# Last two experts' rows gathered in quarters and turned by VectorE, second-layer conversions moved, wider planned steps for the later searches

## The chip, the cores and the metric

One core of one Trainium2 chip runs the whole program. The metric is device time in microseconds (us), the median of several executions. TensorE (PE), VectorE (DVE), ScalarE (ACT), GpSimd (POOL) and SyncE (SP) each run their own queue of instructions in order; a DMA is issued from SP's, ACT's or POOL's queue.

## The reference

Eight heads of causal retention (attention scores with a decay in place of a softmax) give 4608 rows of 512, and a mixture of eight experts works on those rows. Each token goes to one expert, by a greedy walk over all logits from the largest down, 576 tokens per expert.

```python
scores = scale * np.matmul(q, k.transpose(0, 1, 3, 2))      # B, H, S, D = 8, 8, 576, 64
ret = scores * Dmat[None]                                   # Dmat = gamma ** (i - j), i >= j
x = np.matmul(ret, v) ... reshape(4608, 512)
...
order = np.argsort(-(x @ w_gate).flatten())
for idx in order:
    tok, e = int(idx) // E, int(idx) % E
    if assigned[tok] >= 0 or counts[e] >= cap:              # cap = 576
        continue
    assigned[tok] = e; counts[e] += 1
...
for e in range(E):
    mask = assigned == e
    out[mask] = np.maximum(x[mask] @ w1[e], 0.0) @ w2[e]    # 512 -> 1024 -> 512
```

## The kernel before

The first 165 us or so compute the retention and the logits; the rows x are written to a buffer `xd` in HBM. The rest is the mixture, and only this is changed.

**Routing.** The sort is replaced by searches. Phase p (0 to 7) finds the p-th expert to fill up and its 576 tokens. `search` narrows a threshold in seven steps: VectorE makes a table G (line 173), PE counts with it (nine matmuls, line 346, into `r`), VectorE turns the counts into the next table. Then `members` (PE line 414, after a scan `sc` on VectorE, line 405), `listing` (PE line 452, result `idx`: five columns of 128 row numbers) and `leave`, which strikes the tokens out. These phases run beside the experts' matmuls, one or two experts ahead.

**Experts** are numbered 0 to 7 in the order in which the phases find them. `gather` fetches an expert's rows from `xd` by five indirect DMAs on POOL's queue, 128 rows of 2048 bytes each (64 in the last). `transposes` turns them: per 128 rows four PE transposes into PSUM (line 942), a copy `xh` rounded to fp32r on ScalarE (944), and the remainder `xl` by a subtraction on VectorE (945). Weights come as `raw` tiles by SP; `conv` splits one into a high part (ScalarE, 910) and a low part, for which ScalarE writes the negated high part of it (914) and an accumulating DMA on POOL's queue adds `raw` (915). Four conversions of W2 stand in layer 1 of their own expert, four of W1 of the next expert in layer 2.

**Layer 1** (`l1`): 16 groups i = 0 to 15 of 12 matmuls (line 973), over 256 and 320 tokens in turn. ScalarE evicts a group as `hb` (977), VectorE makes its remainder (980). **Layer 2** (`l2`): five tiles of tokens, each in eight steps; a step is three matmuls of 512 columns (line 1014), in the last tile of 64 tokens two. `scatter` writes a tile to the output by an indirect DMA on POOL's queue. So an expert has 192 + 112 = 304 matmuls.

**Order.** The order on each engine is fixed when the program is written, by `Mixer`: `t` is a planned time of PE that `adv` moves on with every three matmuls, `v` a planned time of VectorE; a phase yields how long VectorE needs before its next PE instructions, multiplied by `slack` (1.0 for p < 2, else 1.2), and these are put into PE's queue when `t` has come so far. In layer 2 a step counts 650 ns in every tile.

Of the kernel before, what the change touches and what calls it, by code (L numbers as in the profile page):

```python
# [10 lines left out]
F32 = mybir.dt.float32  # L11
F32R = mybir.dt.float32r
BF16 = mybir.dt.bfloat16
I32 = mybir.dt.int32
ALU = mybir.AluOpType
AF = mybir.ActivationFunctionType
# [3 lines left out]
NP, HP, NB = 4, 4, 9  # L20
N, DM, E, FF = 4608, 512, 8, 1024
SLACK = 1.0

def consts_np():
    h = np.arange(H); g = (1.0 - 2.0 ** (-5.0 - h)).astype(np.float64)
# [61 lines left out]
class Route:  # L87
# [333 lines left out]
    def listing(s, p):  # L421

        nc, V, pool, ps = s.nc, s.nc.vector, s.pool, s.ps
        q = s.q
        lb, hb = pool.tile([128, 36, 2], BF16, name="lb"), pool.tile([128, 36], BF16, name="hb16")

        V.tensor_scalar(hb, q, 1.5*2**28, 1.5*2**28, op0=ALU.add, op1=ALU.subtract)
        two = lambda a: a[:, :, None].to_broadcast([128, 36, 2])
        V.scalar_tensor_tensor(lb, two(q), HALF, two(hb), op0=ALU.add, op1=ALU.subtract)

        rh = pool.tile([128, 3, 20, 36], BF16, name="rh")
        lc = ps.tile([128, 168], F32, name="r")
        lp, cn = lc[:, :160].rearrange("p (v x c) -> p v x c", v=2, c=4), lc[:, 160:]
        early = 0 < p < E - 1
        w = 4 if p else 2
        if early:
            s.taken()
        for g0, g1 in ((0, 9),) if p else ((0, 5), (5, 9)):
            c, n = slice(4*g0, 4*g1), 4*(g1 - g0)
            V.tensor_tensor(rh[:, 2, :, c], s.i20[:, :, c], hb[:, None, c].to_broadcast([128, 20, n]), op=ALU.is_equal)  # L440
            s.reach(4*g0, 4*g1, 32, lb, ALU.is_equal)
            if p:
                V.tensor_scalar(rh[:, 1, :, c], rh[:, 2, :, c], s.pc, None, op0=ALU.mult)
            else:
                nc.scalar.activation(rh[:, 1, :, c], rh[:, 2, :, c], AF.Copy, scale=s.pc)
            V.tensor_tensor(rh[:, 0, :, c], rh[:, 2, :, c], s.cc[:, :, c], op=ALU.mult)
        if not p:
            s.idle(9)
        for g0, g1 in ((0, 9),) if p else ((0, 5), (5, 9)):
            yield (2500 if not p else 3700 if early else 2780), (75 if p else 110)*(g1 - g0)  # L450
            for c in range(4*g0, 4*g1, w):
                nc.tensor.matmul(lp[:32*w, :, :, :w], s.G[:, c:c+w].rearrange("p c k -> p (c k)"), rh[:, 0:2, :, c:c+w],
                                 start=(c == 0), stop=(c + w == 36), skip_group_check=True)
        if early:
            nc.tensor.matmul(cn, s.ones, s.n8, start=True, stop=True, skip_group_check=True)
        if early:
            s.room(cn)
        s.idx = pool.tile([128, 5], I32, name="idx", bufs=8)
        lo = pool.tile([32, 2, 2, 20], F32, name="lo")
        own = [lp[32*c:32*c+32, :, :, c] for c in range(4)]  # L460
        for c in range(w//2):
            V.tensor_copy(lo[:, c], own[c])
        for a, b in ((0, own[2]), (1, own[3]), (0, lo[:, 1])) if w == 4 else ((0, own[1]),):
            V.tensor_tensor(lo[:, a], b, lo[:, a], op=ALU.add)
        for a in range(4):
            V.scalar_tensor_tensor(s.idx[32*a:32*a+32], lo[:, 0, 0, 5*a:5*a+5], 128.0, lo[:, 0, 1, 5*a:5*a+5], op0=ALU.mult, op1=ALU.add)

    def taken(s):

# [390 lines left out]
def moe(tc, nc, P, R, xd, w1_d, w2_d, out, mix):  # L860
    V, A, T = nc.vector, nc.scalar, nc.tensor
    ident, warm = P['ident'], P['warm']
    found = []
    ready = lambda k: len(found) > k
    regs, XG = {}, {}
    state = dict(dma=0, conv=0, most=2, listing=-1)
    RAW, W1, W2, XH, XL = {}, {}, {}, {}, {}
    scat = []
# [1 line left out]

    def phases():
        for p in range(E):
            mix.slack = 1.0 if p < 2 else 1.2
            if p < E - 1:
                yield from (R.search() if p else R.search_first())
                regs[p] = nc.sync.value_load(R.e[0:1, 0:1], min_val=0, max_val=E - 1)
            state['listing'] = p
            yield from R.members(p)
            if p == E - 1:
                regs[p] = nc.sync.value_load(R.e[0:1, 0:1], min_val=0, max_val=E - 1)  # L880
            yield from R.listing(p)
            found.append(R.idx)
            if p == 0:
                yield 0, 0
            if p < E - 1:
                yield from R.leave(p)

    def dma_pump():

        while state['dma'] < min(state['conv'] + 4, 8*E):  # L890
            e, k = divmod(state['dma'], 8)
            if e not in regs or state['dma'] >= state['most']:
                return
            t = P['raw']()
            src = (w1_d if k < 4 else w2_d)
            nc.sync.dma_start(t, src[bass.ds(regs[e], 1), :, (k % 4)*1024:(k % 4)*1024+1024].rearrange("a p x -> (a p) x"))
            RAW[e, k] = t
            state['dma'] += 1
# [18 lines left out]
        state['conv'] += 1  # L917
        dma_pump()

    def gather(e):  # L920
        if e in XG or not ready(e):
            return
        xg = P["c"].tile([128, 5, DM], F32, name="xg", tag="xg")
        for j in range(5):
            n = 128 if j < 4 else 64
            nc.gpsimd.indirect_dma_start(out=xg[:n, j, :], out_offset=None, in_=xd[:, :],  # L926
                                         in_offset=bass.IndirectOffsetOnAxis(ap=found[e][:n, j:j+1], axis=0))
        XG[e] = xg
        state['arrives'] = mix.t + 9000

    def transposes(e):

        xg = XG[e]
        xh = P['w'].tile([128, 4, 576], F32R, name="xh", bufs=1)
        xl = P['w'].tile([128, 4, 576], F32R, name="xl", bufs=1)
        XH[e], XL[e] = xh, xl
        for j in range(5):
            n = 128 if j < 4 else 64
            tag = ("t", "h0", "h1", "h0", "h1")[j] if e else ("t", "y", "y", "t", "y")[j]
# [9 lines left out]
    def l1(e, tr):  # L949
# [4 lines left out]
            order[:8] = [(f, s) for s in range(2) for f in range(4)]  # L954
        for i, (f, s) in enumerate(order):
            wh, wl = [w.rearrange("p (f d m) -> p f d m", f=2, d=4)[:, f % 2] for w in W1[e, f // 2]]
            if i == 0 and e:
                next(tr, None)
                next(tr, None)
            elif e == 0 and i in (1, 2):  # L960
                next(tr, None)
            elif i in (1, 3):
                for _ in tr:
                    pass
            xh, xl = XH[e], XL[e]
# [16 lines left out]
            mix.vec(340 + 140*s)  # L982
            if e == 0 and i == 4:
                state['most'] = 8*E
            if i in ((3, 5, 9, 13) if e else (3, 5, 7, 9, 11, 13)):
                conv()
        return hb

# [8 lines left out]
    def l2(e, hb):  # L997
# [41 lines left out]
            conv()  # L1039
        if e + 1 < E and e + 1 not in XH:  # L1040
            mix.drain(lambda: ready(e + 1))
            gather(e + 1)
            tr = transposes(e + 1)
        return tr

# [24 lines left out]
    run.regs = regs  # L1070
    return run

def build(tc, nc, qk, vk, cst, wg, rf, w1, w2, out):
    with ExitStack() as top:
        P = {}
        P['c'] = top.enter_context(tc.tile_pool(name="c", bufs=1))
# [21 lines left out]
        with ExitStack() as ctx:  # L1098
# [15 lines left out]
                if what:  # L1114
                    warm(what)
            R.idle = idle
            run = moe(tc, nc, P, R, xd, w1, w2, out, mix)
            mix.drain(lambda: 0 in run.regs)
            while rows:
                rows.pop(0)()  # L1120
# [21 lines left out]
```

## Time and profile before

| | us |
|---|---|
| median of 3 runs | 637.7 (636.39 to 641.17) |
| profiled execution | 638.66 |
| its span (first to last instruction) | 636.9 |
| PE / DVE / ACT / POOL busy | 606.7 / 394.4 / 265.5 / 222.7 |

The span and all busy times are of the one profiled execution; 1.76 us of its time lie outside the span. Matmuls overlap, so a busy PE is not a PE at its peak: a row's duration (0.39 us for a matmul of 512 columns) is longer than the distance to the next one.

### The profile page before, as it was taken

Reading aid. Unit: us, or ns where it says so; the run is one execution under the profiler, and the core shown is the slowest. Engines: PE = TensorE matmul, PEld = TensorE weight load, DVE = VectorE, ACT = ScalarE, POOL = GpSimd, SP = SyncE. Lnnn points to the kernel's source line nnn. Section 1 sums busy time; section 2 is a strip of 40 time slices with the busy share of each in tenths; the row PEclk is TensorE's granted clock in tenths of the full one; section 3 lists DMA queues with packets and bytes.
Section 4 is the critical chain, followed back from the end, with each engine's and each line's share of the span. In section 5 each row is a group of like instructions: output and inputs, shape, how many; then the busy total and the mean of one; then the engine's idle time right before and its main releaser. Section 6 shows DMA issues by size and latency. Waiting matters only on the chain.

```text
span 636.9 us, 14773 instructions
## 1 busy us (share of the span) xinstructions
PE 606.7 (95%) x5758; PEld 520.1 (82%) x5762; DVE 394.4 (62%) x1444; ACT 265.5 (42%) x455; POOL 222.7 (35%) x268
## 2 busy tenths in 40 slices
PE   7999999998899999999999999979999999999995
PEld 5888888765598779878977987879789889889973
DVE  2466788788789878878976996878682203302300
ACT  1333333342364445543562465155415724734510
POOL 4887374600311352251432323151323224131111
PEclk9999999999999999999999999999999999999998
DMA  8999898934667597894897399467938986893521
GB/s 328 410 381 373 283 392 259 365 106 142 199 162 170 184 248 179 235 240 140 210 226 233 81 234 241 125 148 189 249 118 187 204 263 144 192 264 95 100 59 41
DMA packets 53368, 133.73 MB, mean 210 GB/s; under 512 B 7026, under 2 KB 22258, under 8 KB 53298
## 3 DMA queue, kind: packets, MB, share of 16 engines
q0 software_dynamic: 14816, 51.39, 37.0%
q1 hardware_dynamic: 38338, 81.14, 36.4%
q8 instruction: 45, 0.74, 0.5%
q10 hardware_dynamic: 144, 0.26, 0.1%
q14 instruction: 25, 0.20, 0.1%
HBM read 81.39 MB, written 18.87 MB: 157 GB/s over the span
## 4 chain that ended last, share of the span: by engine, by line
PE 70%; DVE 12%; DMA 7%; issue 6%; ACT 2%; POOL 2%; SPq 1%; POOLq 0%; ACTq 0%; DVEq 0%
PE ph L973 27%; PE py L1014 25%; PE sc L577 4%; PE px L621 3%; PE pS L598 2%; PE px L612 2%; PE r L346 2%; PE pt L942 2%; DMA qin<-in_qk 2%; DMA vin<-in_vk 1%; DMA xd<-raw 1%; DMA w2l<-raw 1%; PE pT L653 1%; DVE G L173 1%; DMA nin<-in_vk 1%
## 5 line engine op out<-in xcount | busy, mean ns | idle before, releaser
L1014 PE MATMUL py<-w2h,hb 128*128 128x512 f32 x576 | 188.3, 399 | 0.0
L973 PE MATMUL ph<-xh,w1h 128*128 128x320 f32 (+1 forms) x512 | 152.5, 301 | 1.7 <-ACT xh L944 1.0
L973 PE MATMUL ph<-xl,w1h 128*128 128x320 f32 (+1 forms) x512 | 149.7, 296 | 2.2 <-DVE xl L945 1.2
L973 PE MATMUL ph<-xh,w1l 128*128 128x320 f32 (+1 forms) x512 | 149.5, 296 | 0.0
L1014 PE MATMUL py<-w2l,hb 128*128 128x512 f32 (+1 forms) x320 | 125.6, 393 | 1.0 <-DMA w2l<-raw 1.0
L1014 PEld LDWEIGHTS py<-w2h,hb 128*128 128x128 f32 x576 | 104.0, 188 | 20.7
L973 PEld LDWEIGHTS ph<-xh,w1h 128*128 128x128 f32 x512 | 96.3, 189 | 3.7 <-ACT xh L944 1.7
L973 PEld LDWEIGHTS ph<-xl,w1h 128*128 128x128 f32 x512 | 96.5, 190 | 2.5 <-DVE xl L945 1.4
L973 PEld LDWEIGHTS ph<-xh,w1l 128*128 128x128 f32 x512 | 96.4, 190 | 0.5 <-issue 0.5
L977 ACT ACTIVATE hb<-ph 128x256 fp32r<-128x256 f32 (+1 forms) x128 | 51.5, 409 | 107.2 <-PE ph L973 100.0
L980 DVE SCALAR_TENSOR_TENSOR hb<-ph,hb 128x256 fp32r<-128x256 f32 (+1 forms) x192 | 58.7, 351 | 58.4 <-ACT hb L977 53.5
L991 POOL DMA_INDIRECT out_y<-yt,idx x40 | 41.0, 1025 | 119.4 <-ACT yt L1031 76.8
L915 POOL DMA_DIRECT2D w2l<-raw x32 | 28.8, 900 | 115.8 <-ACT hb L977 110.0
L1014 PEld LDWEIGHTS py<-w2l,hb 128*128 128x128 f32 (+1 forms) x320 | 56.7, 177 | 15.3 <-DMA w2l<-raw 2.7
L586 DVE TENSOR_TENSOR am<-sc,cst 128x1024 f32<-128x1024 f32 x32 | 39.1, 1222 | 44.3 <-PE sc L577 44.1
L926 POOL DMA_INDIRECT xg<-xd,idx x40 | 41.5, 1036 | 68.9 <-DMA raw<-in_w 35.7
L1031 ACT ACTIVATE yt<-py 128x512 f32<-128x512 f32 x32 | 19.1, 598 | 106.3 <-PE py L1014 79.5
L562 POOL TENSOR_TENSOR qin<-qin,cst 128x512 f32<-128x512 f32 (+1 forms) x48 | 48.3, 1033 | 39.4 <-DMA qin<-in_qk 33.7
L601 ACT ACTIVATE st<-pS,cst 128x128 f32<-128x128 f32 x64 | 23.5, 367 | 83.1 <-PE pS L598 83.1
L1034 DVE TENSOR_TENSOR yt<-yt,py 64x512 f32<-64x512 f32 x8 | 5.4, 679 | 70.5 <-ACT yt L1033 70.4
L915 POOL DMA_DIRECT2D w1l<-raw x30 | 26.7, 903 | 61.2 <-ACT w1l L914 42.1
L577 PE MATMUL sc<-qin,kin 64*128 64x128 f32 x512 | 39.0, 294 | 1.9 <-POOL qin L562 1.9
(181 smaller groups left out, 919.3 us busy)
## 6 DMA issues: line engine op xcount, KB each, us to landing
raw<-in_w SPq DMA_DIRECT2D x64, 512.0 KB, 5.8
w2l<-raw POOLq DMA_DIRECT2D x32, 512.0 KB
w1l<-raw POOLq DMA_DIRECT2D x30, 512.0 KB
qin<-in_qk SPq DMA_DIRECT2D x14, 576.0 KB
kin<-in_qk SPq DMA_DIRECT2D x14, 576.0 KB
vin<-in_vk SPq DMA_DIRECT2D x14, 576.0 KB, 9.2
nin<-in_vk SPq DMA_DIRECT2D x14, 512.0 KB, 7.6
xd<-raw SPq DMA_DIRECT2D x36, 128.0 KB, 5.9
```

The costliest lines, as they stand in the source:

```text
L562: nc.gpsimd.tensor_tensor(x, x, e[:, None, :n].to_broadcast([128, (b-a)//n, n]), op=ALU.mult)
L577: nc.tensor.matmul(t[:, h, 128*j:128*j+128], blk(k, 4*g+j)[r], blk(q, 4*g+j)[r], start=(j == 0), stop=True, skip_group_check=True)
L586: nc.vector.tensor_tensor(a, SC[u, g].rearrange("p h (j q) -> p h j q", q=128), m1[:, u % HP, :, None, :].to_broadcast([128, 2, 4, 128]), ...
L601: nc.scalar.activation(s, p, AF.Copy, scale=ss[:, u % HP, c:c+1])
L621: nc.tensor.matmul(PX[u, g][y:y+64, b, 128*c:128*c+128], blk(v, 4*g+j)[:, 64*h:64*h+64], AM[u, g][:, h, j], start=False, stop=True, skip_g ...
L915: nc.gpsimd.dma_start(lo, raw, accum_op=ALU.add)
L926: nc.gpsimd.indirect_dma_start(out=xg[:n, j, :], out_offset=None, in_=xd[:, :], in_offset=bass.IndirectOffsetOnAxis(ap=found[e][:n, j:j+1] ...
L973: T.matmul(ps, w, x, start=(k == 0), stop=(k == 11))
L977: A.activation(hb[:, f, c], ps, AF.Relu)
L980: V.scalar_tensor_tensor(hb[:, f, to+a:to+b], ps[:, a:b], 0.0, hb[:, f, 256*s+a:256*s+b].bitcast(F32), op0=ALU.max, op1=ALU.subtract)
L991: st = nc.gpsimd.indirect_dma_start(out=out[:, :], out_offset=bass.IndirectOffsetOnAxis(ap=found[e][:n, t:t+1], axis=0), in_=y[:n], in_off ...
L1014: T.matmul(ps[:m], a, w, start=(k == 0), stop=(k == last), skip_group_check=True)
```

## The change

Three things, in lines of `listing`, `phases`, `dma_pump`, `gather`, `transposes` and `l1`.

Experts 6 and 7 (`PIECES = 6`): `xd` is read as rows of 512 bytes (a quarter of a token's row). `listing` makes a second index, `quarter`, and 18 indirect DMAs each fetch four quarters of 32 tokens, a quarter to each 32 partitions. They are put into POOL's queue one by one, 1300 ns of planned time apart. VectorE then turns blocks of 32x32 into `xz` in SBUF; ScalarE and VectorE make `xh` and `xl` from that. Since features lie in another order then, W1 of these experts is read from a second copy, `in_w1n`. PE has no transposes for them.

The conversions of W2 for experts 1 to 7 stand after groups i = 2, 4, 7 and 10 of layer 1, not 3, 5, 9 and 13. And `slack` is 1.35 for p >= 4.

```diff
+        if p >= PIECES:
+            s.quarter = pool.tile([128, 20], I32, name="quarter", bufs=2)
+            V.tensor_scalar(lo[:, 1], lo[:, 0], 4.0, None, op0=ALU.mult)
+            for a in range(4):
+                V.scalar_tensor_tensor(s.quarter[32*a:32*a+32], lo[:, 1, 0], 128.0, lo[:, 1, 1], op0=ALU.mult, op1=ALU.add)
+                if a:
+                    V.tensor_scalar(s.quarter[32*a:32*a+32], s.quarter[32*a:32*a+32], float(a), None, op0=ALU.add)
...
-            mix.slack = 1.0 if p < 2 else 1.2
+            mix.slack = 1.0 if p < 2 else 1.2 if p < 4 else 1.35
...
-            src = (w1_d if k < 4 else w2_d)
+            src = ((w1_d[0] if e < PIECES else w1_d[1]) if k < 4 else w2_d)
...
-    def gather(e):
+    def gather(e, all=False):
         if e in XG or not ready(e):
+            return
+        if e >= PIECES:
+            if e not in parts:
+                parts[e] = P["c"].tile([128, 18, 128], F32, name="xg", tag="xg"), [(4*x + a, 5*a + x) for x in range(5) for a in range(4 if x < 4 else 2)]
+                state['piece'] = mix.t
+            t, left = parts[e]
+            while left and (all or state['piece'] <= mix.t):
+                k, v = left.pop(0)
+                nc.gpsimd.indirect_dma_start(out=t[:, k, :], out_offset=None, in_=xq[:, :],
+                                             in_offset=bass.IndirectOffsetOnAxis(ap=quarters[e][:, v:v+1], axis=0))
+                state['piece'] = mix.t + 1300
+            if not left:
+                XG[e] = t
+                state['arrives'] = mix.t + 6000
             return
...
+        if e >= PIECES:
+            low = []
+            for j in range(5):
+                n = 128 if j < 4 else 64
+                z = P['w'].tile([128, 4, 128], F32, name="xz", bufs=2)
+                V.transpose(z[:, :, :n].rearrange("p h (s j) -> p h s j", j=32), xg[:, 4*j:4*j+n//32].rearrange("p s (h i) -> p h s i", i=32))
+                o, l = [x[:, :, j*128:j*128+n] for x in (xh, xl)]
+                A.activation(o, z[:, :, :n], AF.Copy)
+                low.append(lambda z=z, n=n, o=o, l=l: V.tensor_tensor(l, z[:, :, :n], o.bitcast(F32), op=ALU.subtract))
+                mix.vec(700)
+                if j:
+                    low.pop(0)()
+                    mix.vec(610)
+                yield
+            low.pop(0)()
+            return
...
+            if i == 0 and e >= PIECES:
+                for _ in tr:
+                    pass
...
-            if i in ((3, 5, 9, 13) if e else (3, 5, 7, 9, 11, 13)):
+            if i in ((2, 4, 7, 10) if e else (3, 5, 7, 9, 11, 13)):
```

Line numbers of the changed kernel are higher, by 1 to 45. Three places in the order of instructions follow.

PE at the start of expert 6's layer 2, before (`pt` are the transposes for expert 7; five such blocks stand between steps):

```order
L973 MATMUL ph<-xh,w1l 128x320
L1014 MATMUL py<-w2h,hb 128x512 x2
L1014 MATMUL py<-w2l,hb 128x512
L942 MATMUL pt<-ident,xg 128x128 x4
L1014 MATMUL py<-w2h,hb 128x512 x2
```

The same place now:

```order
L1017 MATMUL ph<-xh,w1l 128x320
L1058 MATMUL py<-w2h,hb 128x512 x2
L1058 MATMUL py<-w2l,hb 128x512
L1058 MATMUL py<-w2h,hb 128x512 x2
L1058 MATMUL py<-w2l,hb 128x512
```

The transposes are gone from PE here and in expert 5's layer 2.

POOL's queue from the end of expert 5 to layer 2 of expert 6, before (`out_y` is a scatter, `xg` the gather for expert 7):

```order
L991 DMA out_y<-yt,idx 4608x512
L926 DMA xg<-xd,idx 128x512 x4
L926 DMA xg<-xd,idx 64x512
L915 DMA w2l<-raw 128x1024 x4
L915 DMA w1l<-raw 128x1024 x2
```

And now:

```order
L1035 DMA out_y<-yt,idx 4608x512
L941 DMA xg<-xd,quarter 128x128 x3
L926 DMA w2l<-raw 128x1024
L941 DMA xg<-xd,quarter 128x128 x2
L926 DMA w2l<-raw 128x1024
L941 DMA xg<-xd,quarter 128x128 x3
L926 DMA w2l<-raw 128x1024
L941 DMA xg<-xd,quarter 128x128 x3
L926 DMA w2l<-raw 128x1024
L941 DMA xg<-xd,quarter 128x128 x6
L926 DMA w1l<-raw 128x1024
L941 DMA xg<-xd,quarter 128x128
```

Eleven of the 18 pieces now stand ahead of the fourth `w2l`. In expert 5 the row is one `w2l`, one piece, then `w2l`, three pieces, `w2l`, three pieces, `w2l` and the other eleven among the rest; in expert 3 the gather for expert 4 stands ahead of the third `w2l`, before it stood ahead of the second.

DVE in expert 4's layer 1, from the end of `leave` (`oh`) to the first table G of p = 6, before (`hb` rows are the remainders of layer 1's groups, two or three rows a pair of groups):

```order
L219 TENSOR_TENSOR oh<-t_446,mx_447 128x288
L1034 TENSOR_TENSOR yt<-yt,py 64x512
L980 SCALAR_TENSOR_TENSOR hb<-ph,hb 128x256 x2
L980 SCALAR_TENSOR_TENSOR hb<-ph,hb 128x64
L161 TENSOR_SCALAR om<-m 128x36
L163 TENSOR_TENSOR om<-m,om 128x36
L167 TENSOR_SCALAR dg<-om 128x36
L332 CAST v<-dg 128x72
L173 TENSOR_TENSOR G<-ct,v 128x1152
```

And now:

```order
L220 TENSOR_TENSOR oh<-t_446,mx_447 128x288
L1024 SCALAR_TENSOR_TENSOR hb<-ph,hb 128x256 x2
L1024 SCALAR_TENSOR_TENSOR hb<-ph,hb 128x64
L1024 SCALAR_TENSOR_TENSOR hb<-ph,hb 128x256 x2
L1024 SCALAR_TENSOR_TENSOR hb<-ph,hb 128x64
L162 TENSOR_SCALAR om<-m 128x36
L164 TENSOR_TENSOR om<-m,om 128x36
L168 TENSOR_SCALAR dg<-om 128x36
L333 CAST v<-dg 128x72
L174 TENSOR_TENSOR G<-ct,v 128x1152
```

The table comes two groups later behind its listing. On PE the listing for p = 5 moves from (3,302), that is after 302 of expert 3's 304 matmuls, to (4,75), and the first count of p = 6 from (4,54) to (4,153); the listing for p = 4 moves from (3,57) to (3,96), the first count of p = 5 from (3,120) to (3,174). The member matmul of p = 6 moves from (4,249) to (5,6), its listing from (4,273) to (5,51), that of p = 7 from (5,27) to (5,174). Up to the first count of p = 4, at (2,192) before and (2,195) now, PE's order is as it was.

## Rows read from the trace of the kernel before

**Rows 1.** The page, part 1: busy us (share of the span) and instructions.

```profile
PE 606.7 (95%) x5758; PEld 520.1 (82%) x5762; DVE 394.4 (62%) x1444; ACT 265.5 (42%) x455; POOL 222.7 (35%) x268
```

**Rows 2.** Busy time by stretch: expert 6's layer 2, expert 7's, expert 6's layer 1.

```profile
core 0: us, PE busy (x) PEld busy (x) DVE busy (x) ACT busy (x) POOL busy (x), PEclk, DMA share, GB/s
549.89:577.79 27.90, 27.90 (x135) 22.09 (x134) 3.62 (x8) 12.85 (x18) 8.37 (x14) 1.00 0.92 236
603.37:629.50 26.13, 25.85 (x114) 20.33 (x112) 0.61 (x3) 2.83 (x5) 4.87 (x10) 1.00 0.21 61
524.31:549.89 25.58, 25.58 (x193) 25.58 (x192) 7.71 (x23) 13.74 (x24) 8.78 (x10) 1.00 0.66 155
```

**Rows 3.** Waits of PE from 170 us: us in total, times, longest.

```profile
PE r L346 <- DVE G L173: 4.8, 6, 1.6
...
PE ph L973 <- issue: 1.0, 1, 1.0
...
PE py L1014 <- DMA w2l<-raw: 1.0, 2, 0.7
```

**Rows 4.** Timeline of PE, start of expert 6's layer 2: start, us.

```profile
549.89 0.63 PE L1014 MATMUL py<-w2h,hb 128*128 128x512 f32 x2
...
550.59 0.46 PE L942 MATMUL pt<-ident,xg 128*128 128x128 f32 x4
550.88 0.69 PE L1014 MATMUL py<-w2h,hb 128*128 128x512 f32 x2
...
556.14 0.63 PE L1014 MATMUL py<-w2h,hb 128*128 128x512 f32 x2
```

**Rows 5.** Groups of VectorE and ScalarE by form: count, busy us, mean ns, idle before.

```profile
L674 DVE STREAM_TRANSPOSE raw<-xT 128x512 f32<-128x512 f32 x27 | 17.6, 686 | 1.1 <-DMA xd<-raw 1.1
...
L945 DVE TENSOR_TENSOR xl<-pt,xh 128x512 fp32r<-128x512 f32 x32 | 20.5, 684 | 6.5 <-ACT xh L944 6.2
...
L944 ACT ACTIVATE xh<-pt 128x512 fp32r<-128x512 f32 x32 | 17.8, 598 | 12.9 <-PE pt L942 12.8
```

**Rows 6.** Timeline of PE, places of searches, 347 to 470 us.

```profile
347.61 0.39 PE L346 MATMUL r<-oh,G 128*128 128x32 bf16 x9 [0.17 <-PE py L1014]
...
367.42 0.39 PE L346 MATMUL r<-oh,G 128*128 128x32 bf16 x9 [0.28 <-DVE G L173]
...
372.05 0.39 PE L346 MATMUL r<-oh,G 128*128 128x32 bf16 x9 [0.23 <-DVE G L173]
...
407.18 0.84 PE L452 MATMUL r<-rh,G 128*128 128x160 bf16 x9
...
416.80 0.39 PE L346 MATMUL r<-oh,G 128*128 128x32 bf16 x9 [1.09 <-DVE G L173]
...
423.22 0.31 PE L973 MATMUL ph<-xl,w1h 128*128 128x320 f32 x1 [0.99 <-issue]
...
429.35 0.39 PE L346 MATMUL r<-oh,G 128*128 128x32 bf16 x9 [1.60 <-DVE G L173]
...
469.31 0.18 PE L414 MATMUL r<-sc,cb 128*128 128x2 bf16 x1 [0.40 <-DVE sc L405]
```

**Rows 7.** Timeline of VectorE: a member scan, and a remainder near the stall.

```profile
351.55 0.31 DVE L405 TENSOR_TENSOR_SCAN sc<-mem 128x72 bf16<-128x72 f32 x1
...
425.93 0.42 DVE L980 SCALAR_TENSOR_TENSOR hb<-ph,hb 128x256 fp32r<-128x256 f32 x1 [1.61 <-ACT hb L977]
```

**Rows 8.** Timeline of PE: the two waits for w2l, experts 2 and 7.

```profile
326.73 0.50 PE L1014 MATMUL py<-w2l,hb 128*128 128x512 f32 x1 [0.67 <-DMA w2l<-raw]
...
608.37 0.50 PE L1014 MATMUL py<-w2l,hb 128*128 128x512 f32 x1 [0.28 <-DMA w2l<-raw]
```

**Rows 9.** Timeline of POOL: gathers, and the fourth w2l of experts 2 and 7.

```profile
317.88 1.29 POOL L926 DMA_INDIRECT xg<-xd,idx  x1 [0.30 <-issue]
319.18 1.01 POOL L915 DMA_DIRECT2D w2l<-raw  x1
...
527.35 1.01 POOL L926 DMA_INDIRECT xg<-xd,idx  x1 [0.31 <-issue]
...
602.99 0.86 POOL L915 DMA_DIRECT2D w2l<-raw  x1 [5.54 <-ACT hb L977]
```

More of the change, by code (lines that the diff above doesn't have):

```diff
@@ L22 @@
 SLACK = 1.0
+PIECES = 6
 def consts_np():
@@ L864, in moe @@
     ready = lambda k: len(found) > k
-    regs, XG = {}, {}
+    regs, XG, quarters, parts = {}, {}, {}, {}
+    xq = xd.rearrange("n (a c) -> (n a) c", a=4)
     state = dict(dma=0, conv=0, most=2, listing=-1)
@@ L882, in phases @@
             found.append(R.idx)
+            if p >= PIECES:
+                quarters[p] = R.quarter
             if p == 0:
@@ L1041, in l2 @@
             mix.drain(lambda: ready(e + 1))
-            gather(e + 1)
+            gather(e + 1, True)
             tr = transposes(e + 1)
@@ L1071, in moe, with build @@
     return run
-def build(tc, nc, qk, vk, cst, wg, rf, w1, w2, out):
+def build(tc, nc, qk, vk, cst, wg, rf, w1, w1n, w2, out):
     with ExitStack() as top:
@@ L1116, in build @@
             R.idle = idle
-            run = moe(tc, nc, P, R, xd, w1, w2, out, mix)
+            run = moe(tc, nc, P, R, xd, (w1, w1n), w2, out, mix)
             mix.drain(lambda: 0 in run.regs)
@@ L1129 @@
     w1 = np.asarray(moe_w1).reshape(E, HP, 4, 32, 8, 128).transpose(0, 1, 3, 4, 2, 5).reshape(E, 128, 4096)
+    w1n = np.asarray(moe_w1).reshape(E, HP, 128, 8, 128).transpose(0, 2, 3, 1, 4).reshape(E, 128, 4096)
     w2 = np.asarray(moe_w2).reshape(E, 8, 128, DM).transpose(0, 2, 1, 3).reshape(E, 128, 4096)
-    arrays = dict(in_qk=qk, in_vk=vk, in_cst=consts_np(), in_wg=moe_w_gate, in_rf=route_consts(), in_w1=w1, in_w2=w2)
+    arrays = dict(in_qk=qk, in_vk=vk, in_cst=consts_np(), in_wg=moe_w_gate, in_rf=route_consts(), in_w1=w1, in_w1n=w1n, in_w2=w2)
     arrays = {n: np.ascontiguousarray(x) for n, x in arrays.items()}
```

## The prediction

> **What bounds the kernel now.** I read the page's first part, then busy time by stretch, the waits of TensorE, and last the timelines around each wait. TensorE is busy 95% of the span [rows 1]. Experts are numbered 0 to 7 in the order in which the routing finds them; each costs 192 matmuls of layer 1 and 112 of layer 2, and a place such as (4,54) means "after 54 of expert 4's 304". A layer 1 without a wait takes 25.58 us, and PE, its weight loads too, is busy for all of it [rows 2]: pairs of groups of 12 take 25.58/8 = 3.2 us, so a matmul takes 0.133 us on average. The last layer 2 takes 26.13 us, 25.7 without its one wait, so 0.23 us a matmul. From 170 us on PE waits for little: 4.8 us in six waits for the table G of a search, 1.0 us for w2l, 1.0 us that the profile can't assign [rows 3]. So a gain can only come from matmuls taken out and from those few waits; whatever VectorE, ScalarE, GpSimd and the DMAs do more costs nothing until it ends such a wait. The clock stands at 1.00 in these stretches [rows 2].
>
> **Transposes of experts 6 and 7: -4.3 us.** Before, five blocks of four transposes stand between the first six steps of layer 2. A step of three matmuls is 0.69 us; the six steps from 549.89 to 556.14 take 6.25 us instead of 6 x 0.685 = 4.1 [rows 4]: 2.15 us. The whole layer 2 says the same, 27.90 against 25.7 us, 2.2 [rows 2]. Two experts lose them: 4.3 us, all on TensorE's path.
>
> What comes instead lies on VectorE and ScalarE. A turn of 128x512 took 0.69 us on VectorE, the subtraction 0.68 and ScalarE's copy 0.60 [rows 5] (subtraction and copy read PSUM there and will read SBUF, so the price is an estimate). Five pieces take VectorE 5 x 1.37 = 6.9 us, in a layer 2 where it is busy for 3.62 of 27.90 us [rows 2], and the five subtractions that read PSUM, some 3 us of that, are gone. Eight small operations on 32 rows make the new indices, the second time after the last search. I cost both at nothing; uncovered they would be 7 us per expert, at the first matmul that reads xl.
>
> **Eighteen gathers instead of five, on GpSimd's queue.** A gather of 128 rows holds GpSimd 1.01 us with 0.31 before the next [rows 9]; 128 pieces of 512 bytes are 128 descriptors as well, so I take 1.25 to 1.3 us each, 23 us per expert instead of 6.4. None is on TensorE's path itself. Queued behind them are the accumulating w2l and w1l transfers and the scatters. The tightest place is the fourth w2l, needed 20 matmuls (4.6 us) into layer 2. A w2l is issued 2.8 us after its group ends (the one issued at 602.99 follows the group that ended 3.2 us before layer 1's end at 603.37) and is used 5.4 to 7.5 us later (602.99 to 608.37, and 319.18 to 326.73 with a gather beside it) [rows 8, 9]. In expert 6 eleven pieces and three w2l go first: issue at 20.3 us of layer 1, landing by 25.7 to 27.8, needed at 30.2. In expert 5 the list is there only at about 12.5 us; seven pieces go first, issue at 23.4, landing by 28.8 to 30.9, needed at 31.3. The last piece lands about 8 us before expert 6's layer 1. In expert 3 the gather for expert 4 now comes later and stands ahead of the third w2l: landing by 29 to 31, needed at 32.2. All fit, two with under 1.5 us to spare at the long end; I put 0.4 us of new wait there, bounds 0 and 1.5.
>
> VectorE can slow these issues: the row at 317.88 took 1.29 us, while listing work ran on VectorE [rows 9]. The Trainium skill's page "SBUF — State Buffer" (the box on the "DVE blocks DMA" trap) speaks against putting more gathers beside VectorE: while VectorE runs in a mode with both ports, GpSimd can't write descriptors. The slow row agrees with that without proving it. If all 18 pieces took that row's 1.29 + 0.30 us, expert 5's w2l would come 7 x 0.3 = 2.1 us later and expert 6's 11 x 0.3 = 3.3: up to 3 us lost together.
>
> **Second layer's conversions sooner: -0.4 us.** After groups 3, 5, 8 and 11 instead of 4, 6, 10 and 14. Of the two w2l waits one goes: at 608.37 PE waited 0.28 us and the next matmul took 0.11 us longer [rows 8], and the fourth conversion is now 4.8 us sooner. The other (0.67 us at 326.73) stays: there the w2l was issued at 319.18, the moment the five gathers of expert 3 left the queue [rows 9], and they stand ahead of it still. ScalarE's conversions, 2 us each, only change places; a search step that follows the next group's subtraction pays up to 1 us on VectorE, and by the new positions only steps with slack have that. With the 0.4 us above this nets to 0.
>
> **More margin for the searches: -1.8 us.** From p = 4 on the waits are 0.17, 0.28, 0.23, 1.09 and 0.40 [rows 6], 2.2 us, with 0.1 for each restart 2.7. The largest is the first table after a listing: 9.6 us from listing to table (407.18 to 416.80), PE gave it (3,302) to (4,54), 56 matmuls. Now it gets 78 (10.4 us plus the listing's own 0.95). The same holds at expert 3 (78 instead of 63). What is late next is the step across the end of a layer 2, whose last tile has half the matmuls that the planner counts: from (4,292) to (5,6) are 12 x 0.23 + 6 x 0.12 + 0.3 = 3.8 us, and from the last count to the member scan VectorE needs 4.25 (347.61 to the scan's end at 351.86) [rows 6, 7]: a new wait of 0.45, with two small ones and restarts 0.9. Ends: 0 and -2.7. Everything before (2,192) stands where it stood.
>
> **A stall that is nobody's.** At 423.22 PE idles 0.99 us for no shown reason; ScalarE's evictions shift with it, VectorE waits 1.61 us for one, and the table at 429.35 is 1.60 us late [rows 6, 7]: 2.6 us. Without the stall that table would come about 0.1 us late, so the change's margin is not what would save it. The profiled execution (638.66 us, a span of 636.90 and 1.76 around it) lies 1.0 over the median of 637.7, and without the stall it would be 636.1, under the fastest of the three. I count half of it, 1.3 us, as gone.
>
> **Sum**: 638.66 - 4.3 - 1.8 - 0 - 1.3 = 631.3; from the median, 637.7 - 6.1 = 631.6, and with the stall gone for good 630.0. I say **631.0**.
>
> **Rivals.**
> 1. The margin only moves the waits. VectorE has the same work for p = 4 to 6 and its searches' steps come later, where conversions and subtractions crowd them. Against: the longest wait (1.09) gets 22 matmuls more. Then -4.3 + 0.4 remain: 633.8.
> 2. Slower: GpSimd's queue. If a 512-byte piece cost much more than a 128-row gather, the fourth w2l of experts 5 and 6 comes late by 7 and 11 times the surplus, less some 5 us of slack together. At 1.9 us a piece that eats the 6.1 us; at 2.3 it is 18 x 1.05 - 5 = 14 us lost: 645. Against: the issue time goes with descriptors, 1.01 us for 128 [rows 9], and those stay 128. The Trainium skill's page "DMA: Bandwidth & Descriptors" (Anatomy of one DMA — SWDGE path) gives each such DMA a fixed 2.0 us; one behind another, 64 KB pieces would take 2.15 us by that estimate, and the kernel 642. The trace bears it out only in part: the next gather is issued 1.3 us after the one before, so the fixed parts overlap.
> 3. Larger gain: the stall goes for good, and p = 4 to 6 wait nowhere. -4.3 - 2.7 - 0.4 - 2.6: 628.7.
>
> **Chances.** Forecast (629.3 to 632.6) 0.55; rival 1 0.25; rival 3 0.15; rival 2 0.05. The range 628.2 to 634.6 takes in rivals 1 and 3 and leaves out the second, and the ends of the w2l bound. About 1% (6.4 us, below 631.3) is what a measurement of this kernel can tell from no change; the forecast lies on that line: a bit more than half of it and all of rival 3 give 0.48 faster, 0.47 within, 0.05 slower.
>
> **What would show it.** No transposes in experts 5's and 6's layer 2 and both at about 25.7 us; the two layers 1 after them at 25.6, without a wait for xl. Gathers some 1.3 us apart. No wait at 608's w2l, that of expert 2 still there, and at most small ones at (5,212) and (3,206). Tables G of p = 5 and 6 without a wait over 0.5 us, and one for the member scan at (5,6). I am wrong if PE waits for w2l or xl in experts 5 to 7 for over 1.5 us, or if the search waits sum to 2 us again.

## The result and the profile after

The changed kernel takes 630.94 us (median of four runs, 629.99 to 633.08), the kernel before 638.84 (four runs, 636.39 to 641.17): a ratio of 0.9875, 95% interval 0.9842 to 0.9909, so faster by 1.25% (0.9 to 1.6). Forecast: 631.0. The profiled execution after has a span of 629.4 us. Place names and expert numbers are the prediction's; L941 is a gather of a quarter, L951 one of whole rows, L926 an accumulating transfer.

The page of the changed kernel, part 1 (columns as in [rows 1]):

```profile
PE 601.2 (96%) x5722; PEld 517.5 (82%) x5722; DVE 405.0 (64%) x1470; ACT 265.6 (42%) x455; POOL 249.0 (40%) x294
```

TensorE has 36 records fewer (40 transposes less, and some records missing in either trace) and 5.5 us less to do, GpSimd 26 instructions and 26 us more. Next, busy time by stretch in the changed kernel: layer 2 of experts 5, 6 and 7, and expert 6's layer 1 (columns as in [rows 2]):

```profile
492.20:517.69 25.49, 25.49 (x114) 20.60 (x113) 7.85 (x19) 13.01 (x18) 17.25 (x22) 1.00 0.89 226
543.28:568.76 25.48, 25.48 (x114) 20.60 (x113) 6.38 (x12) 12.95 (x18) 12.09 (x18) 1.00 0.95 253
594.35:619.84 25.49, 25.49 (x114) 20.41 (x112) 0.56 (x2) 2.83 (x5) 4.38 (x8) 1.00 0.11 42
517.69:543.28 25.59, 25.59 (x194) 25.59 (x192) 7.96 (x23) 13.85 (x24) 18.69 (x19) 1.00 0.81 199
```

All three layers 2 now cost the same 25.5 us: 27.90 in [rows 2] has lost its transposes. The layer 1 of expert 6, the first that reads turned rows, stays at 25.59 us, so nothing waits for them. The timeline of PE at the start of expert 6's layer 2 shows steps of 0.69 us one behind another, where [rows 4] has a block of four transposes between them:

```profile
543.28 0.63 PE L1058 MATMUL py<-w2h,hb 128*128 128x512 f32 x2
543.74 0.39 PE L1058 MATMUL py<-w2l,hb 128*128 128x512 f32 x1
543.97 0.62 PE L1058 MATMUL py<-w2h,hb 128*128 128x512 f32 x2
```

What took their place, groups of VectorE and ScalarE by form (columns as in [rows 5]):

```profile
L967 DVE STREAM_TRANSPOSE xz<-xg 128x512 f32<-128x512 f32 x8 | 5.6, 704 | 0.4 <-DMA xg<-xd,quarter 0.3
L970 DVE TENSOR_TENSOR xl<-xz,xh 128x512 fp32r<-128x512 f32 x8 | 5.3, 660 | 17.7 <-ACT w1l L925 10.5 <-ACT xh L969 7.2
...
L969 ACT ACTIVATE xh<-xz 128x512 fp32r<-128x512 f32 x8 | 4.8, 627 | 3.3 <-DVE xz L967 2.7 <-issue 0.7
```

704, 660 and 627 ns, against the estimates of 0.69, 0.68 and 0.60 us. Waits of PE from 170 us on, changed kernel (us in total, times, longest; compare [rows 3]: G has halved, the wait for nothing shown is 0.2 instead of 1.0, and those for w2l, [rows 8], are gone):

```profile
PE r L347 <- DVE G L174: 2.5, 3, 1.2
PE ph L1017 <- DVE xl L986: 1.9, 2, 1.2
PE ph L1017 <- ACT xh L985: 0.7, 1, 0.7
PE r L415 <- DVE sc L406: 0.3, 1, 0.3
PE ph L1017 <- issue: 0.2, 1, 0.2
```

Two of the three waits for G stand in the part that nothing moved; the third, at (4,186), is new. So is the one for the member scan at (5,6), 0.33 us (0.45 was predicted). Timeline of PE, the two new ones:

```profile
433.72 0.34 PE L347 MATMUL r<-oh,G 128*128 128x32 bf16 x7 [0.90 <-DVE G L174]
...
465.51 0.18 PE L415 MATMUL r<-sc,cb 128*128 128x2 bf16 x1 [0.33 <-DVE sc L406]
```

GpSimd's queue (compare [rows 9]): pieces that follow one another start 1.25 to 1.35 us apart, with accumulating transfers between some of them (timeline of POOL, changed kernel, expert 7's gather).

```profile
526.38 1.04 POOL L941 DMA_INDIRECT xg<-xd,quarter  x1 [0.30 <-issue]
527.72 0.98 POOL L941 DMA_INDIRECT xg<-xd,quarter  x1 [0.30 <-issue]
528.66 1.05 POOL L926 DMA_DIRECT2D w2l<-raw  x1
530.02 1.05 POOL L941 DMA_INDIRECT xg<-xd,quarter  x1 [0.30 <-issue]
```

The line that no step of the prediction looked at is at the end of the program. It is GpSimd's closing drain, in the view of the program's last line (duration ns: min, median, max; the max is the closing one), first before, then after:

```profile
L1136 POOLq DRAIN  x3: 46/107/5012, 631.0 to 636.6; - x3
```

```profile
L1181 POOLq DRAIN  x3: 46/107/7172, 621.4 to 629.1; - x3
```

In both kernels it starts some 0.2 us ahead of the last scatter's row, and the program ends 0.8 us after it: the drain is 2.16 us longer, and so is the time from the last matmul to the end (7.26 us before, 9.42 after).

### The profile page after: what moved, and what is told of

The parts are those of the page before. It is cut to its first block, busy times and chain, and to the rows that moved or that the text cites. A ratio compares the mean times of both kernels' runs of the same rounds, so it can differ in the third digit from the quotient of the medians.

```text
span 629.4 us, 14756 instructions
## 1 busy us (share of the span) xinstructions
PE 601.2 (96%) x5722; PEld 517.5 (82%) x5722; DVE 405.0 (64%) x1470; ACT 265.6 (42%) x455; POOL 249.0 (40%) x294
## 4 chain that ended last, share of the span: by engine, by line
PE 76%; DVE 10%; issue 6%; DMA 3%; ACT 2%; POOL 1%; SPq 0%; POOLq 0%; ACTq 0%
PE ph L1017 30%; PE py L1058 26%; PE sc L585 4%; PE px L629 3%; PE pS L606 2%; PE px L620 2%; PE r L347 2%; DMA qin<-in_qk 2%; PE pt L983 1%; PE pT L661 1%; DMA raw<-in_w 1%; DMA nin<-in_vk 1%; PE r L453 1%; DVE am L594 1%; DVE G L235 1%
## 5 line engine op out<-in xcount | busy, mean ns | idle before, releaser
L951 POOL DMA_INDIRECT xg<-xd,idx x30 | 30.0, 999 | 80.8 <-DMA raw<-in_w 36.7
L926 POOL DMA_DIRECT2D w2l<-raw x32 | 29.9, 947 | 68.0 <-ACT w2l L925 43.7
L926 POOL DMA_DIRECT2D w1l<-raw x30 | 27.5, 930 | 54.3 <-ACT w1l L925 44.3
L941 POOL DMA_INDIRECT xg<-xd,quarter x36 | 36.0, 1001 | 14.1 <-issue 10.0
```

The costliest lines, as they stand in the source:

```text
L926: nc.gpsimd.dma_start(lo, raw, accum_op=ALU.add)
L941: nc.gpsimd.indirect_dma_start(out=t[:, k, :], out_offset=None, in_=xq[:, :], in_offset=bass.IndirectOffsetOnAxis(ap=quarters[e][:, v:v+1] ...
```

## Experiments

The table gives what the comparisons rest on, in us. Stretches run from one layer's first matmul to the next layer's, in each kernel's timeline of PE; "matmuls" is from the first of layer 1 of expert 0 to the last. The first stands between 168.1 and 174.6 us in these executions, after the same code, so the stretches tell more than the spans. Each ratio is to runs of the kernel before on the same chip, whose medians go from 635.0 us (beside g1) to 638.9, so times from different rows compare less well than ratios.

| kernel | us, ratio to before (95%) | matmuls | L1 of 4 | L2 of 5 | L2 of 6 | drain |
|---|---|---|---|---|---|---|
| before | 638.8 | 459.5 | 31.47 | 27.82 | 27.89 | 5.01 |
| changed | 630.9, 0.9875 (0.9842–0.9909) | 448.7 | 28.21 | 25.49 | 25.49 | 7.17 |
| e1 pieces | 644.3, 1.0114 (1.0075–1.0154) | 460.8 | 31.43 | 28.51 | 28.56 | 7.17 |
| e2 margin | 631.8, 0.9888 (0.9863–0.9913) | 451.5 | 27.15 | 27.68 | 27.67 | 5.01 |
| e3 conversions | 634.9, 0.9933 (0.9905–0.9961) | 455.7 | 29.77 | 27.67 | 27.67 | 5.01 |
| e4 one expert | 633.2, 0.9913 (0.9879–0.9948) | 450.6 | 28.27 | 27.66 | 25.49 | 6.07 |
| e5 26 gathers | 652.2, one run | 470.5 | 31.50 | 27.67 | 27.67 | 6.97 |
| e6 26 plain | 640.2, one run | 458.1 | 31.47 | 27.69 | 27.67 | 6.98 |
| e7 gather later | 634.7, 0.9939 (0.9915–0.9962) | 453.6 | 28.46 | 27.67 | 27.68 | 5.14 |
| e8 pieces, margin | 632.6, 0.9902 (0.9855–0.9950) | 450.5 | 27.14 | 26.68 | 27.21 | 7.18 |
| f1 | 644.3, 1.0103 (1.0086–1.0120) | 463.5 | 27.14 | 25.55 | 25.49 | 6.19 |
| f2 | 637.4, 0.9983 (0.9968–0.9997) | 454.3 | 26.96 | 25.49 | 25.49 | 7.26 |
| f3 changed again | 630.6, 0.9895 (0.9874–0.9915) | 448.6 | 28.29 | 25.49 | 25.49 | 7.18 |
| g1 | 629.6, 0.9916 (0.9889–0.9942) | 447.9 | 27.15 | 25.49 | 25.49 | 6.52 |

**The three parts, each alone.** The pieces and the turn by VectorE (e1), with the two lines of the others left as before:

```
 mix.slack = 1.0 if p < 2 else 1.2
 if i in ((3, 5, 9, 13) if e else (3, 5, 7, 9, 11, 13)):
```

> The kernel before with experts 6 and 7 gathered in quarters and turned by VectorE, nothing else. Theory (the parts add up): layer 2 of experts 5 and 6 takes 25.5 us instead of 27.8, so 4.7 us go there; but GpSimd's last drain, 5.0 us before and 7.2 in the changed kernel, grows with the 26 more DMAs on its queue and gives 2.1 us back: 2.6 us faster, about 0.4%. Rival (the longer end is chance or belongs to another part): the drain stays at 5 us and the kernel is 4.7 us faster.

Slower by 1.1%: both theories failed. The transposes are gone, but layer 2 of experts 5 and 6 is longer than with them. Waits of PE in e1 (us in total, times, longest), and the first of the two in PE's timeline:

```profile
PE py L1058 <- DMA w2l<-raw: 5.5, 2, 2.8
```

```profile
504.66 0.50 PE L1058 MATMUL py<-w2l,hb 128*128 128x512 f32 x1 [2.73 <-DMA w2l<-raw]
```

That is the queue of rival 2, and it needs no dear piece: with the conversions after groups 4, 6, 10 and 14, the fourth w2l stands behind the pieces and comes 2.7 us late at the usual 1.25 to 1.35 us each.

There is a second price, in layer 2 of expert 4 (31.6 us, before 30.0). The member scan waits 2.01 us there; before, the same scan waited 0.40 ([rows 6], 469.31). Between that scan and the listing ahead of it stand the small operations for expert 6's `quarter`, from 463.69 to 465.2 us on VectorE. PE in e1, and two rows of VectorE:

```profile
470.30 0.18 PE L415 MATMUL r<-sc,cb 128*128 128x2 bf16 x1 [2.01 <-DVE sc L406]
```

```profile
463.69 0.17 DVE L470 TENSOR_SCALAR lo<-lo 32x40 f32<-32x40 f32 x1
463.90 0.35 DVE L472 SCALAR_TENSOR_TENSOR quarter<-lo 32x20 int32<-32x20 f32 x2
```

By stretches e1 is 1.3 us worse on the matmuls and 2.2 in the drain. That is 3.5 of the 5.9 us that lie between the medians; the profiled execution of e1 is its fastest.

The margin alone (e2):

```
-mix.slack = 1.0 if p < 2 else 1.2
+mix.slack = 1.0 if p < 2 else 1.2 if p < 4 else 1.35
```

> The kernel before with slack 1.35 for p >= 4, nothing else. Theory: waits for tables G from p = 4 on fall from 3.8 us (1.6 of it behind the late evictions at 423 us) to about 1.2; PE's time from (2,192) to the start of expert 5's layer 2 falls by 2 to 4 us, the end stays at 5.0 us of drain; 2 to 4 us faster. Rival (the margin only moves waits): under 1 us.

6.5 us by the medians (638.35 to 631.81), more than any theory gave it, and 8.0 by the stretch of all matmuls. Of these 8.0, 4.3 stand in layer 1 of expert 4; another part is the two waits for w2l of [rows 8], 0.95 us, which e2's execution doesn't have.

The conversions alone (e3):

```
-if i in ((3, 5, 9, 13) if e else (3, 5, 7, 9, 11, 13)):
+if i in ((2, 4, 7, 10) if e else (3, 5, 7, 9, 11, 13)):
```

> The kernel before with the W2 conversions after groups 2, 4, 7 and 10, nothing else. Theory: the w2l wait of expert 7 goes (0.4 us) and that of expert 2 stays, since its transfer is queued behind a gather; within 1 us of before. Rival: both go (1.2 us), since the transfer needs ScalarE earlier and not POOL, or search steps wait more on VectorE (up to 1 us slower).

Faster by 0.7%, and again in layer 1 of expert 4 (31.47 to 29.77), where the prediction had them change nothing. The waits for w2l of [rows 8] are gone here. With the old places they come and go: of the nine traces with old places in experts 1 to 4, six have a wait of 0.2 to 0.7 us for a fourth w2l in expert 1, 2 or 7 (before, e5, e6, e8, f1, g1). That of expert 7 comes in two of the seven traces that have the old place there (before, and 0.21 us in e5). None of the five traces with the new places has one. So the order has a part in them, though no single execution shows it. Timelines of PE, expert 7 in e5 and expert 2 in f1:

```profile
619.96 0.50 PE L1025 MATMUL py<-w2l,hb 128*128 128x512 f32 x1 [0.21 <-DMA w2l<-raw]
```

```profile
326.14 0.50 PE L1058 MATMUL py<-w2l,hb 128*128 128x512 f32 x1 [0.37 <-DMA w2l<-raw]
```

Pieces and margin, without the conversions (e8: the changed kernel with the "-" line of e3):

> The changed kernel with the conversions of the second layer's weights at their old places. Theory (what the move of the conversions does is to cover the pieces): the waits of TensorE for the fourth w2l of experts 5 and 6 are there as in e1, 2 to 3 us each, expert 4's layer 1 is at 27.2 us where the changed kernel has 28.2, and the drain stays at 7.17: about 4 us slower than the changed kernel, 635 us (ratio 0.994). Rival (the margin alone clears GpSimd's queue, the conversions' move is idle): no wait above 0.5 us for w2l, and 1 us faster than the changed kernel, 630 us.

Between the two theories. The waits for w2l are back, 0.90 and 1.40 us, and the two layers 2 are together 2.9 us longer than in the changed kernel; in return layer 1 of expert 4 is 1.1 us shorter. So the conversions' move pays for the pieces (net 1.8 us on the matmuls), by being out of the queue before them; the total, with its wide interval, doesn't show it.

**The drain.** Pieces for the last expert alone (e4):

```
-PIECES = 6
+PIECES = 7
```

> The changed kernel with pieces for expert 7 alone. Theory: expert 5's layer 2 is 2.3 us longer again, the drain is about 6.1 us, half-way between 5.0 and 7.2: 1.2 us slower than the changed kernel. Rival (the drain doesn't count DMAs): drain 5 or 7, so 0.1 or 2.3 us slower.

6.07 us, half the growth, as expected; layer 2 of expert 5 keeps its transposes (27.66 us), and by stretches the kernel is 1.9 us worse on the matmuls and 1.1 better in the drain. To see which DMAs count, the kernel before got 26 more, first with an index list (e5), then without (e6):

```
+if 1 <= e <= 5 and i % 3 == 1 and i > 3 and more:      # twice
+    nc.gpsimd.indirect_dma_start(out=extra[0][:, x, :], in_=xs[:, :], ...)   # e5: 128 rows x 16 B
+    nc.gpsimd.dma_start(extra[0][:, x, :], xs[128*x:128*x+128, :])           # e6
```

> The kernel before with 26 more indirect gathers on GpSimd (128 rows of 16 bytes each, into a scratch tile that nobody reads), two at a time in layer 1 of experts 1 to 5: as many GpSimd DMAs as the pieces add, and none of them in experts 6 and 7. Theory (the closing drain of GpSimd grows by 83 ns for every DMA that GpSimd issued, worked out from 5.01, 6.07 and 7.17 us at 0, 13 and 26 more): the drain lasts 7.17 us, and the end comes 2.16 us later after the last matmul. Rival (the drain grows because the pieces are gathered near the end, or because of their 128 x 512 bytes): it stays at 5.01 us.

> As e5_more_gathers, but the 26 more are plain DMAs of 128 rows of 16 bytes on GpSimd's queue, without an index list. If every DMA of GpSimd counts, the drain lasts 7.17 us; if only those with an index list count, it stays at 5.01 us.

```profile
L1147 POOLq DRAIN  x3: 46/107/6974, 642.6 to 650.1; - x3
```

```profile
L1146 POOLq DRAIN  x3: 46/107/6976, 630.6 to 638.2; - x3
```

Both (e5, then e6) 6.97 us: every DMA that GpSimd issues counts, wherever it stands, 75 ns each here and 83 in the changed kernel. The rival falls. What nobody expected is e5's time: its matmuls take 11 us longer than before, those of e6 don't. The bytes are the same, 53 KB; what differs is the index list, and with it GpSimd's time: a small gather follows the one before after 1.25 us, four plain DMAs take 2.23 us together. From 319.0 to 325.3 us the last row gather and four small ones stand one behind another on GpSimd, and VectorE idles 4.07 us of that, up to 325.28, for TensorE work that had long ended.

**The stall in expert 4.** In the kernel before, [rows 6, 7] show PE and ScalarE stopping near 423 us. The row of ScalarE there, and GpSimd's queue beside it (timelines of before):

```profile
418.93 0.38 ACT L977 ACTIVATE hb<-ph 128x256 fp32r<-128x256 f32 x1 [1.57 <-PE ph L973]
423.29 0.44 ACT L977 ACTIVATE hb<-ph 128x320 fp32r<-128x320 f32 x1 [3.98 <-PE r L346]
```

```profile
415.87 1.01 POOL L926 DMA_INDIRECT xg<-xd,idx  x1 [0.30 <-issue]
...
421.04 1.29 POOL L926 DMA_INDIRECT xg<-xd,idx  x1 [0.30 <-issue]
422.32 1.01 POOL L915 DMA_DIRECT2D w2l<-raw  x1
```

The group that the second eviction reads had ended at 419.76; the eviction comes 3.5 us late, 1 us after the last of five gathers in a row. e7 takes expert 5's gather out of expert 4's layer 1:

```
-    gather(e + 1)
+    if e != 4:
+        gather(e + 1)
```

> The kernel before, in which expert 5's rows are gathered in expert 4's layer 2 and no longer in its layer 1. Theory (the late ScalarE eviction at 423 us, with the 0.99 us stall and the 1.60 us wait for table G behind it, comes from the five gathers that GpSimd runs at 415.9 to 422.3 us): the eviction of expert 4's group 5 is on time, expert 4's layer 1 takes 28.7 to 29.0 us where it took 31.4, and the whole about 2.5 us less (ratio 0.996), with up to 0.5 us given back where the transposes of expert 5 come later. Rival (the stall belongs to the search's steps, whose margin is too small there): layer 1 of expert 4 stays within 0.3 us of 31.4.

31.47 to 28.46 us, and the eviction is on time; the table at (4,54) still waits 1.10 us, which is the search's own. e1, e3 and e6, with the old margin, have the stall at the same place (PE waits of 0.8, 1.0 and 1.0 us for "issue"), so it belongs to the order.

**Towards a better kernel.** f1: the changed kernel with the conversions sooner in experts 5 and 6 only, and twelve low parts by VectorE.

```
-if i in ((2, 4, 7, 10) if e else
+if i in ((2, 4, 7, 10) if e > 4 else (3, 5, 9, 13) if e else
-if fast:
+if fast or e >= 7 or (e == 6 and k >= 4):
```

> The changed kernel with two edits that show in different stages. (a) The conversions stand sooner only in experts 5 and 6 (where the pieces are); experts 1 to 4 have their old places. (b) The last 12 low parts of the weights (second layer of expert 6, both layers of expert 7) are made by a VectorE subtraction and no longer by an accumulating DMA of GpSimd. Theory: (a) what the move of the conversions costs, 1.06 us in expert 4's layer 1, goes (28.21 to 27.15 us), and experts 5 and 6 keep 25.5 us in layer 2 without a wait for w2l; (b) 12 DMAs fewer shorten GpSimd's closing drain by 12 x 0.083 = 1.0 us (7.17 to 6.17 us). Together 2.0 us less than the changed kernel, ratio to the kernel before 0.984. Rival to (a): the wait in expert 4 stays and the fourth w2l of experts 2 to 4 comes late as well, no gain. Rival to (b): VectorE, with 12 subtractions of 128 x 1024 more, holds the evictions of experts 6 and 7 and gives 1 us or more back there.

Both sides that were counted came (27.14 us in expert 4, a drain of 6.19), and the kernel is 1% slower than before: layer 1 of expert 6 takes 40.5 us. With expert 6's four accumulating transfers gone from the queue, expert 7's 18 pieces stand in one row. The stretch in f1 and a part of it (columns as in [rows 2]), PE's waits and ScalarE's in the whole:

```profile
515.86:556.37 40.51, 32.96 (x194) 30.48 (x193) 12.59 (x27) 10.28 (x20) 19.50 (x20) 0.79 0.33 114
531.90:549.00 17.10, 11.98 (x43) 10.28 (x43) 3.89 (x10) 3.98 (x8) 8.34 (x10) 0.50 0.22 70
```

```profile
ACT hb L1021 <- remote: 15.7, 3, 6.7
...
PE ph L1017 <- issue: 7.4, 12, 1.6
```

The mean granted clock was 0.79 there. TensorE was busy without a break up to 527.3 us and for 2.17 of the next 4.6; from 531.9 to 549.0 us the granted clock stood at 0.50, the lower of its two levels (1.2 GHz), which adds to the price. VectorE, between its few instructions, has up to 6.5 us for which no reason is shown. f1 also puts VectorE's subtractions among those pieces. Subtractions alone do no harm: expert 7's layer 1 in f1 has them and no gather beside it, and takes 25.59 us without a late eviction. Whether the pieces alone would do it, f1 can't tell.

f2: whole-row gathers of experts 1 to 5 one at a time; their rows count as landed 6 us of planned time after the last gather, not 9.

```
+while left and (all or e == 0 or state['piece'] <= mix.t):
+    j = left.pop(0); nc.gpsimd.indirect_dma_start(...)
+    state['piece'] = mix.t + 2600
```

> The changed kernel with the row gathers of experts 1 to 5 issued one at a time, at least 2.6 us of planned time apart, instead of five in a row. Theory (it is five gathers in a row on GpSimd beside which ScalarE's evictions come late): no eviction is over 1 us late in experts 2 to 4, expert 4's layer 1 takes 27.2 us where the changed kernel takes 28.2, 1 us less in all (ratio to the kernel before 0.986). Rival (any gather on GpSimd does it, or the wait is the conversions' own): expert 4's layer 1 stays at 28.2 us, or a single eviction is late in more places, and the time is within 0.5 us of the changed kernel's.

Here and below an eviction's lateness is the time in which its group has ended and ScalarE stands idle; time behind ScalarE's own conversions is not counted. In experts 2 to 4 the largest is 0.71 us, and layer 1 of expert 4 takes 26.96 us, as the theory has it. But expert 1's rows now arrive late: its layer 1 takes 35.5 us (28.4 before), with waits of up to 2.35 us and the granted clock at 0.50 from 233.3 to 243.5, so the whole is slower than the changed kernel. The rival is out for the evictions; as a version it is no use.

f3 was the changed kernel again, on the same chip:

> The changed kernel once more, as the measure for the two others on the same chip: 630 to 632 us, ratio to the kernel before 0.986 to 0.989 by either theory, GpSimd's closing drain 7.17 us.

630.6 us and a drain of 7.18; the ratio, 0.9895, is a shade over the range.

g1 joins what had worked, and puts a memset between gathers:

```
+nc.gpsimd.memset(spacer, 0.0)          # ahead of each gather
 nc.gpsimd.indirect_dma_start(out=xg[...
-if i in ((2, 4, 7, 10) if e else
+if i in ((2, 4, 7, 10) if e > 4 else (3, 5, 9, 13) if e else
-if fast:
+if fast or e >= 7:
```

> The changed kernel with (a) the conversions sooner only in experts 5 and 6, as in f1, (b) the low parts of expert 7's weights alone by VectorE (8 accumulating DMAs fewer; the second layer of expert 6 keeps its four, which stand among expert 7's pieces), and (c) a GpSimd memset of one element ahead of every gather, as the kernel has it ahead of its scatters. (a) and (b) as f1 measured their good sides: expert 4's layer 1 at 27.1 us, the drain at 7.17 - 8 x 0.083 = 6.5 us, and no row of more than 7 gathers, so expert 6's layer 1 back at 25.6 us: 1.7 us less than the changed kernel (ratio to the kernel before 0.986). For (c), theory: what stops the engines is indirect DMAs that follow one another on GpSimd with nothing between, so with the memsets no eviction of ScalarE is over 1 us late beside gathers. Rival: it is the number of gathers within some microseconds that does it, whatever stands between: evictions stay 1 to 2.4 us late beside the gathers of experts 2 to 4.

From 170 us on not one eviction of layer 1 is over 0.4 us late, while the changed kernel run again has five between 0.6 and 2.5 us. In experts 2 to 4 f1 differs from g1 by the memsets alone, and it has four there, of 0.9 to 1.7 us; so it is the memset that ends them. The gather for expert 5 in g1, and ScalarE beside it:

```profile
421.60 1.03 POOL L953 DMA_INDIRECT xg<-xd,idx  x1 [0.26 <-issue]
422.62 0.09 POOL L952 MEMSET spacer<- 1x1 f32 x1
422.93 0.96 POOL L953 DMA_INDIRECT xg<-xd,idx  x1 [0.23 <-issue]
```

```profile
421.84 0.38 ACT L1023 ACTIVATE hb<-ph 128x256 fp32r<-128x256 f32 x1 [1.00 <-PE ph L1019]
423.60 0.44 ACT L1023 ACTIVATE hb<-ph 128x320 fp32r<-128x320 f32 x1 [1.38 <-PE ph L1019]
```

The gathers are as far apart as without the memsets (1.33 us here, 1.31 in the changed kernel), so these cost nothing. By stretches g1 is 1.4 us better than f3: 0.7 on the matmuls, 0.66 in the drain. The ratios, 0.9916 and 0.9895, come from two chips and overlap: that it beats the changed kernel is not shown in the time. What the memset saves in time is not shown either: layers 1 of experts 2 to 4 take 27.15, 27.18 and 27.15 us in g1, and 27.15, 27.18 and 27.14 in f1 without it. It ends the lateness, but with this order nothing waits for those evictions.

## Why the prediction was right

That the time came so close is luck: the margin with the stall gave 3.4 us more than forecast, the drain and the conversions' price took back 3.2 that were not forecast. The mechanism was right for the transposes and for the direction of the margin.

- **Transposes, -4.3 us: right.** 27.82 and 27.89 became 25.49: -4.7; against the 27.67 that most other kernels show, -4.4. VectorE's and ScalarE's share was hidden, as costed. But the small operations for the index, also put at nothing, are hidden only by the margin: 84 matmuls now stand between the listing and the member scan behind them, (5,51) to (5,135), instead of 29. With the old margin they are nearly all of the 1.6 us by which PE waits longer there (e1).
- **Eighteen pieces hidden on GpSimd: right on the path of the matmuls, for a reason given to another part.** The new w2l wait put at 0.4 us is 0, but only with the conversions' new places, from which the positions were worked out; without them PE waits 2.3 us for w2l (e8), and 5.5 with the old margin too (e1), where the kernel is slower than before. Rival 2 had the right mechanism and the wrong condition: a dear piece. A piece follows the one before after 1.25 to 1.35 us; the 2.3 us at which that rival decided did not come. The reason given against that rival, that the issue time goes with descriptors, is hardly borne out: in the changed kernel a gather of 64 rows holds GpSimd for 0.90 to 0.92 us, one of 128 rows for 0.94 or more. What holds is that the bytes don't matter: 35 of the 36 pieces took 0.94 to 1.05 us. The last took 1.45, so the loss of up to 3 us did not come, beside which the prediction named the Trainium skill's page "SBUF — State Buffer" (the box on the "DVE blocks DMA" trap). Nor did the 642 us that it worked out by the fixed 2.0 us of the Trainium skill's page "DMA: Bandwidth & Descriptors" (Anatomy of one DMA — SWDGE path): at 1.25 to 1.35 us from piece to piece the fixed parts overlap.
- **Missed: the drain, +2.16 us.** The prediction followed each added DMA to its landing and to who is queued behind it, and did not ask who waits for the queue to close. The last line of the program is on the path always.
- **Conversions, 0 net: wrong.** The wait at 608 us went, as forecast, but it comes in only two of seven traces with the old place, so little was to be had; the one of expert 2 that was to stay isn't there after the change. What the move does is to cover the pieces; its price is 1.06 us in expert 4. There the conversion after group 11 stands right behind an eviction that is 2.3 us late (427.53 us); the next eviction follows the 2 us of the conversion, VectorE's remainder waits 1.74 us for it, and the table at (4,186) comes 0.90 us late. f1 and g1, with the old place in expert 4, have 27.14 and 27.15 us.
- **Margin, -1.8, and half of the stall, -1.3: undersized.** Together -3.1; measured alone, -6.5 (e2). The wrong step is "I count half of it": it took the stall for chance, because the profiled time lay above the median. It returns in each kernel with the old order there, and it is worth 3.0 us in layer 1 of expert 4 (e7). Counted whole it would have made -4.4; part of the rest may be the waits for w2l that e2's execution lacks, what more there is stays open. The prediction also held that the margin is not what would save the stall. The margin does save it, by moving the search's steps, so that the late eviction stands where nobody needs it: late evictions are still there in e2, of up to 2.5 us. Also e3 escapes part of it in this way. That the searches' waits would fall was right; rival 1 (margin only moves the waits) is out, and the wait at (5,6) came, 0.33 us for 0.45.

The terms that the runs gave: -4.4 to -4.7 (transposes), -6.5 (margin and stall), +1.1 (conversions in expert 4), +2.2 (drain) make -7.6 to -7.9; the medians say -7.9. They come from different kernels, with intervals of 2 us and more on the totals, so the agreement is no proof that the parts add. By stretches alone, with -8.0 for the margin and stall, the same terms make -9.2 to -9.5, where the two profiles differ by -8.7 from the first matmul to the end.

## What to carry to other kernels

Read the end of the program like any other stage: a change that adds DMAs on one engine's queue pays for them there too, however well each is hidden. A stall that the profile puts down to nobody is not noise until other executions of the same order lack it; look at what the other engines issue at that moment. The other way round, a wait that one execution shows may be missing from the next one with the same order. And cost the parts of a change together: one that gains nothing alone may be what the other stands on, and one that is harmless alone may block it.

## What the runs showed of the hardware

- GpSimd's closing drain took 5.01 us with 142 DMAs issued by it (5.14 in e7), 6.07 with 155, 6.19 with 156, 6.52 with 160, and 6.97 to 7.26 with 168, whether they are indirect or plain, early or late: 75 to 87 ns for each one more. The memsets of g1 (66) don't show in it.
- Beside indirect DMAs that follow one another on GpSimd, other engines stop: an eviction 3.5 us late after five, 15 us lost beside eighteen (f1, with VectorE's subtractions among them and the clock at 0.50 for 17 us of it), 11 us with 26 small ones in groups (e5). A one-element memset between them ended the lateness for rows of five (g1). What stops inside the chip is open: PE shows "issue", ScalarE "remote" or an engine that had long been done. Rows of six pieces in the changed kernel, at 539.80 to 546.20 us, did no harm that PE shows, so the length of the row alone doesn't settle it. That the memset would also mend f1's row of eighteen was not tried.
